# Decode attention and MLP, forward and backward, in one kernel: slots at a multiple of 512 bytes, and the last pass in 133 steps

## The chip, the core and the metric

The kernel runs on one core of a Trainium2 chip. The time is the device time of one execution in microseconds (us); lower is better.

## The reference

Two layers of attention and two of an MLP alternate. Each adds to its input; weights and caches are shared by both layers. B = 2, one query per batch, D = 1024, 32 query heads of 128 that share 4 key/value heads, 16384 cached keys, F = 3584. All arrays are bfloat16. The kernel returns the output and the gradients of all inputs but `B_x`.

```python
def A(x, k_cache, v_cache, wq, wo):           # k, v: [2, 4, 16384, 128]
    q = (x @ wq).reshape(B, 1, 32, 128).transpose(0, 2, 1, 3)
    k, v = repeat(k_cache, 8, axis=1), repeat(v_cache, 8, axis=1)
    p = softmax(einsum("bhqd,bhkd->bhqk", q, k) * 128 ** -0.5)
    return einsum("bhqk,bhkd->bhqd", p, v).transpose(0, 2, 1, 3).reshape(B, 1, 4096) @ wo

def M(x, w1, b1, w2, b2):
    return gelu(layernorm(x) @ w1 + b1) @ w2 + b2

x = x + A(layernorm(x), ...); x = x + M(layernorm(x), ...)   # layer 0
x = x + A(layernorm(x), ...); x = x + M(layernorm(x), ...)   # layer 1
outputs: x, and the vjp of all that with grad_out:
  out_1 = dx, out_2 = dK, out_3 = dV (16.8 million elements each), out_4 = dwq,
  out_5 = dwo, out_6 = dw1, out_7 = db1, out_8 = dw2, out_9 = db2
```

## The kernel before

The program is recorded as a list of pieces (`emit`), each with the chunks of SBUF that it uses, and then run in that order (`Program.run`). A chunk is a megabyte of keys, values or weights, 8 KB in each of 128 partitions. It gets one of 15 slots (or a part of two large tiles, `e1` and `ds1`, while these are free); its load is issued on SP's DMA queue, in the order of first use, as soon as a slot is free. In the last pass three slots are split into halves and four are whole store buffers (`HALF_AT`, `FULL_AT`), so that eight are left for loads. Engines run their instructions in the order in which the pieces stand; they wait for one another by semaphores alone.

There are four passes over the cache: attention forward of layer 0 and 1, backward of layer 1, and backward of layer 0 (`attn_bwd` with `l == 0`, the last pass). A pass goes through 8 groups (batch and key/value head), each in 16 blocks of 1024 cached rows. In a backward pass a step `s` does one value block: `kblock` transposes it on DVE (`kT`, L482) and multiplies it with the gradient (`sc`, L495, two blocks later). When half of a group's blocks is there, `slope` (L977, L980) turns scores into their gradients `ds`, and `xc` (L530) exchanges them across partitions into `xt`. A key block is multiplied with `xt` by `direct` (L520) into `sb[0]`, `LAG_B` = 14 steps behind the value block. `dq_of` (L986) scales the sum into `dq_all`. Only in the last group of the last pass two key blocks are done in a step: steps 126 to 129 and 133 to 136.

The last pass also makes all large outputs. `kv_outputs` writes the gradients of keys and values of both layers at once: eight products of 512 columns (L1180) for each megabyte, from `blk`, a transposed piece of `e` or `ds` (L1162). `dw_units` writes the weight gradients in products of 512 columns (L1234), between rows that `x_rows` (L1218) and `y_rows` (L1198, L1199) have set up in `X` and `Y`. Every product goes into a PSUM bank that `ob()` hands out in turn, `st["ob"] % 3` of `obanks`, and is cast into a store buffer by ACT (L236) or DVE (L239), whichever has less work on the planner's account (`cast_out`). When a buffer is full, POOL's queue issues its store (L1185, L1260).

`outputs(s, ...)` says which of these pieces a step gets: those of `kv_outputs` have their steps, the weight gradients stand in a list `bg`, of which a credit per step takes some. `wq_last_ops` turns the last two chunks of `wq` (L399) and multiplies them with `dq` (L412); `attn_in_bwd` is the backward layer norm (L600 to L616), and `col_to_row` (L562 to L564) writes its result, `out_1`. In the last pass these stand at steps 130 to 142, and steps go on to 149 until nothing is left.

In the forward passes `wo_fwd_blocks` (L648) multiplies the last heads' output with two chunks of `wo`, five steps after the last value chunk's first use.

Of the kernel before, what the change touches and what calls it, by code (L numbers as in the profile page):

```python
# [28 lines left out]
LAG_B = 14  # L29

# [111 lines left out]
def kernel(  # L142
# [71 lines left out]
    def ob():  # L214
        st["ob"] += 1
        return obanks[st["ob"] % 3]
# [337 lines left out]
    def col_to_row(colT, dram_out):  # L554
        c = P.chunk(kind="half")

        def f():
# [6 lines left out]
            GP.dma_start(dram_out, row)  # L564
# [94 lines left out]
    def attn_fwd(l, order, x_in, mark, behind=()):  # L659
# [94 lines left out]
        for i, k in enumerate(kvs):  # L754
# [4 lines left out]
            for n, b in enumerate(wo_fwd_blocks(l, k, xn, i == HKV - 1, acc_x)):  # L759
                at(32 * i + 33 + LAG_F + (n if i + 1 < HKV else 0), *b)  # L760
# [196 lines left out]
    def attn_bwd(l, order, gT, wo_first, outputs=None, mark=None, extra=None):  # L957
# [44 lines left out]
        for pos, g in enumerate(order):  # L1002
            for f in range(2):
                at(16 * pos + 10 + 8 * f, slope(pos, g, f))
                at(16 * pos + 11 + 8 * f, xc(pos, g, f))
            at(137 if l == 0 and pos == G - 1 else 16 * pos + LAG_B + 16, dq_of(pos, g))
# [7 lines left out]
        for i, k in enumerate(kvs):  # L1014
# [16 lines left out]
            else:  # L1031
# [3 lines left out]
                for n, b in enumerate(ops):  # L1035
                    wb.setdefault((118 if l == 1 else 130) + n, []).append(b)

        kc, vc = {}, {}
        n_steps = 128 + LAG_B if l == 1 else 137
        k_at = {}  # L1040
        for v in range(128):
            fast = 126 + v % 16 // 2 if v % 16 < 8 else 129 + v % 16 // 2
            k_at.setdefault(fast if l == 0 and v >= 112 else v + LAG_B, []).append(v)
        s = 0
        while s <= n_steps or (outputs is not None and outputs(s, True)):
            pos, i = divmod(s, 16)
# [3 lines left out]
            fill = list(outputs(s, False)) if outputs is not None else []  # L1050
# [15 lines left out]
            if s < 128:  # L1066
                g = order[pos]
                if i % 4 == 0:
                    kc[0] = ld_kv("V", g, i // 4)
                c = kc[0]  # L1070

                kblock(c, i, scb[0], g, fill[:n] + mids + fill[n:2 * n])
            else:
                for fn, us in fill[:n] + mids + fill[n:2 * n]:
                    emit(fn, us)
                if pend:
                    emit(*pend.pop(0))
            for fn, us in wb.pop(s, []) + (extra or {}).pop(s, []) + fill[2 * n:]:
                emit(fn, us)
            if s == n_steps:  # L1080
                aflush()
                parts = attn_in_bwd(l, gT, dnq)
                if l == 1:
                    for b in tail + parts:
                        emit(*b)
                else:
# [452 lines left out]
```

## Time and profile before

| | us |
|---|---|
| runs before | 1167.36, 1169.02, 1169.89; median 1169.02 |
| the profiled execution, its own time | 1169.38 |
| its span in the trace | 1167.6 |
| busy: PE, DVE, ACT, POOL | 830.9, 770.4, 488.8, 183.4 |
| moved by DMA | 356.5 MB read, 98.6 MB written |

The profile is of one execution. PE is TensorE's matmuls and PEld its weight loads, DVE is VectorE, ACT ScalarE, POOL GpSimd, SP the queue that issues loads. `x16` counts instructions that follow each other; L520 is line 520 of the kernel. Line numbers in the profile are those of the kernel before; in the kernel after, the same lines stand up to eleven further down. The share of the DMA engines counts the time that packets took, as a part of 16 engines' time, and can exceed 1 where packets overlap.

### The profile page before, as it was taken

The numbers are of one execution on the slowest core, as the hardware profiler recorded it, in microseconds if no ns is written. First come the engines' busy times: TensorE is split into PE (matmuls) and PEld (weight loads), VectorE is DVE, ScalarE is ACT, GpSimd is POOL, SyncE is SP. The second block draws the span as 40 slices with busy tenths as digits, with TensorE's granted clock in tenths as the row PEclk, the third lists the DMA queues.
The fourth block names the chain that finished last, engine by engine and source line by source line (L and its number), as shares of the span: only waits on it lengthen the run. The fifth ranks groups of instructions, "written<-read, shape, count | busy, mean of one in ns | idle before, by whom it ended". The sixth has DMA issues, their size and how long they took to land. (4 is left out here: it accounts for less than half of the span.)

```text
span 1167.6 us, 34350 instructions
## 1 busy us (share of the span) xinstructions
PE 830.9 (71%) x14751; PEld 621.6 (53%) x14761; DVE 770.4 (66%) x1490; ACT 488.8 (42%) x1128; POOL 183.4 (16%) x578
## 2 busy tenths in 40 slices
PE   5665565457886546888777578879666987798875
PEld 4554564456775445777767465444333444444443
DVE  5764673269886536664656465979566977787875
ACT  0422223002423221244444206758455866676773
POOL 1000000010000000110111101423222332333341
PEclk9999999999999555577877657989887989798997
DMA  9999999989999999999999997999999999999995
GB/s 356 412 414 414 413 420 410 405 319 413 410 414 414 414 399 356 405 414 412 409 414 412 377 341 275 340 405 424 401 358 407 420 415 381 425 421 399 392 419 218
DMA packets 99636, 457.37 MB, mean 392 GB/s; under 512 B 7668, under 2 KB 11778, under 8 KB 60188
## 3 DMA queue, kind: packets, MB, share of 16 engines
q1 hardware_dynamic: 81660, 356.56, 76.6%
q0 software_dynamic: 17824, 98.63, 20.7%
q8 instruction: 115, 1.88, 0.6%
q14 instruction: 37, 0.30, 0.1%
HBM read 356.54 MB, written 98.62 MB: 390 GB/s over the span
## 5 line engine op out<-in xcount | busy, mean ns | idle before, releaser
L482 DVE STREAM_TRANSPOSE kT<-slot 128x512 int32<-128x512 int32 x480 | 322.3, 694 | 130.3 <-PE sc L495 91.1
L495 PE MATMUL sc<-qbd,kT 128*128 128x32 bf16 x4096 | 264.7, 223 | 14.4 <-DVE kT L482 11.2
L495 PEld LDWEIGHTS <-kT 128*128 128x128 bf16 x4096 | 210.5, 115 | 59.1 <-issue 27.1
L520 PEld LDWEIGHTS <-slot 128*128 128x128 bf16 x3648 | 148.4, 103 | 131.7 <-issue 48.7
L236 ACT CAST slot<-sc 128x512 bf16<-128x512 f32 x332 | 189.0, 593 | 66.2 <-PE sc L1234 32.5
L520 PE MATMUL sb<-xt,slot 128*128 128x8 bf16 x3648 | 165.9, 177 | 65.3 <-DMA slot<-in_A_v_cache_dram 28.9
L239 DVE CAST slot<-sc 128x512 bf16<-128x512 f32 x187 | 126.2, 681 | 37.2 <-PE sc L1180 18.8
L1180 PE MATMUL sc<-slot,blk 128*128 128x512 bf16 x335 | 129.6, 405 | 25.7 <-DVE slot L239 8.4
L711 ACT ACTIVATE e<-sc 128x512 bf16<-128x512 f32 x32 | 19.0, 597 | 253.9 <-DVE sc L708 182.1
L236 ACT CAST slot<-sb 128x512 bf16<-128x512 f32 x169 | 100.0, 592 | 47.6 <-PE sb L1180 27.0
L530 POOL COPY xt<-ds 32x64 int32<-32x64 int32 x368 | 84.7, 230 | 192.1 <-DVE ds L980 155.9
L402 ACT COPY slot<-tp 128x512 int32<-128x512 int32 x96 | 55.2, 586 | 139.8 <-PE tp L399 138.3
L399 PE MATMUL tp<-ident,slot 128*128 128x128 bf16 x832 | 81.4, 264 | 18.0 <-DMA slot<-in_A_wq_dram 12.0
L1180 PEld LDWEIGHTS <-blk 128*128 128x128 bf16 x512 | 45.0, 99 | 69.4 <-issue 57.3
L1180 PE MATMUL sb<-slot,blk 128*128 128x512 bf16 x170 | 68.8, 405 | 17.8 <-DVE slot L239 13.1
L399 PEld LDWEIGHTS <-slot 128*128 128x128 bf16 x832 | 66.9, 121 | 21.9 <-DMA slot<-in_A_wq_dram 12.8
L530 ACT COPY xt<-e 32x128 int32<-32x128 int32 x256 | 75.6, 295 | 3.9
L239 DVE CAST slot<-sb 128x512 bf16<-128x512 f32 x96 | 65.0, 677 | 16.6 <-DMA out_dram<-slot 7.1
L1185 POOL DMA_DIRECT2D out_dram<-slot x64 | 35.3, 551 | 215.7 <-ACT slot L236 178.8
L384 DVE STREAM_TRANSPOSE slot<-slot 128x1024 int32<-128x1024 int32 (+1 forms) x48 | 55.2, 1178 | 15.3 <-DMA slot<-in_A_wq_dram 8.1
L1234 PE MATMUL sc<-slot,X 128*128 128x512 bf16 x157 | 60.7, 407 | 5.5 <-DVE slot L239 3.3
L587 POOL TENSOR_TENSOR m_rstd<-ln_vpe,neghalf 128x2 f32<-128x2 f32 x2 | 1.4, 716 | 374.2 <-DVE ln_vpe L585 374.2
(282 smaller groups left out, 932.9 us busy)
## 6 DMA issues: line engine op xcount, KB each, us to landing
slot<-in_A_k_cache_dram SPq DMA_DIRECT2D x114, 1024.0 KB, 14.4
slot<-in_A_v_cache_dram SPq DMA_DIRECT2D x109, 1024.0 KB, 13.4
out_dram<-slot POOLq DMA_DIRECT2D x64, 1024.0 KB, 11.3
slot<-in_A_wq_dram SPq DMA_DIRECT2D x31, 1024.0 KB, 12.5
slot<-in_A_wo_dram SPq DMA_DIRECT2D x27, 1024.0 KB, 12.5
out_dram<-slot POOLq DMA_DIRECT2D x54, 512.0 KB, 12.5
slot<-in_B_w_dram SPq DMA_DIRECT2D x22, 896.0 KB, 11.0
slot<-in_B_w_dram SPq DMA_DIRECT2D x11, 1024.0 KB, 11.4
```

Source lines behind the costliest of these rows:

```text
L236: S.copy(out=dst, in_=src)
L239: V.tensor_copy(out=dst, in_=src)
L384: V.transpose(out=t.ap[:, h * nw * 256:(h + 1) * nw * 256].bitcast(I32).rearrange("p (w j m) -> p w j m", j=4, m=32), in_=c.ap[:, 0:4 * nc ...
L399: PE.transpose(tp[:, j * 128:(j + 1) * 128], c.ap[:, off + j * 128:off + (j + 1) * 128], ident[:])
L402: S.copy(out=d.bitcast(I32), in_=tp.bitcast(I32))
L482: V.transpose(out=kT[:].bitcast(I32).rearrange("p (w j m) -> p w j m", w=4, j=4), in_=c.ap[:, (i % 4) * 1024:(i % 4 + 1) * 1024].bitcast(I ...
L495: PE.matmul(sc[:, a0:a0 + 4, :, 2 * (i % 4) + q], lhsT=kv[:, 2 * q + w, :, e], rhs=qbd[:, g, 2 * w + e], start=(w == 0 and e == 0), stop=( ...
L520: PE.matmul(acc, lhsT=c.ap[:, n * 128:(n + 1) * 128], rhs=xv[:, i // 4, t // 2, :, 2 * (i % 4) + t % 2], start=(fresh and i == 0 and t == ...
L530: (GP.tensor_copy if on[t % len(on)] == "g" else S.copy)(out=d[32 * t:32 * t + 32, c0:c0 + cn, j, :], in_=s[32 * j:32 * j + 32, c0:c0 + cn ...
L1180: PE.matmul(ps, lhsT=hold["blk"][:, j, :], rhs=flat(qm(w)[:, (u % 2) * 4:(u % 2) * 4 + 4, :]), start=True, stop=True)
L1185: GP.dma_start((dKv if w == 0 else dVv)[g, :, c * 32:(c + 1) * 32, :], stg.ap.rearrange("p (t d) -> p t d", d=128))
L1234: PE.matmul(ps, lhsT=hold[j // 4 * 4][:, j % 4, :], rhs=Y.ap[:, y_at + c0:y_at + c0 + cn], start=True, stop=True)
```

## The change

- **Slots.** `dbias` no longer has an SBUF tile of its own (144 bytes a partition): it uses one named `g_a` that exists. Everything allocated behind it moves down by 160 bytes, so that the first slot starts at byte 104,448 of a partition, a multiple of 512, where it was 104,608.
- **Two blocks a step.** In the last pass the last group's 16 value blocks are done in steps 112 to 119, two a step; its keys in 126 to 133 without the gap; `slope` and `xc` of that group at 117, 118, 122 and 123; its key gradients from step 124; `wq` is turned from step 121.
- **The end.** Steps end at 133 (`N_END`). What is left then is written out in one order by hand: `dq` and its rows, then pieces of the last key gradients, the `wq` products, the weight gradients and the layer norm between each other. `out_1` is stored from SP's queue instead of POOL's, and the layer norm's sums use a part of `sb[0]`.
- **Five banks.** From step 122 on, `obanks` also holds the two banks of the scores.
- **The weight gradients.** The credit changes its constants; the last two sets of `wq` gradients share their `X` rows (`hold_n`); `Y` is cleared before the pass begins, and the rows of `gA_all` are set up only ahead of `out_5`.
- **Forward.** The last two chunks of `wo` are asked for (an empty piece that uses them) one step before the last value chunk.

```diff
 LAG_B = 14
+N_END = 133
...
         st["ob"] += 1
-        return obanks[st["ob"] % 3]
+        return obanks[st["ob"] % len(obanks)]
...
-    def col_to_row(colT, dram_out):
+    def col_to_row(colT, dram_out, queue=None):
         c = P.chunk(kind="half")
...
                 V.tensor_copy(out=row[:, j0 * 128:(j0 + 4) * 128], in_=flat(ps))
-            GP.dma_start(dram_out, row)
+            (queue or GP).dma_start(dram_out, row)
...
             acc_x = (lambda: x_in()[:]) if i == 0 else (lambda: xn[:])
-            for n, b in enumerate(wo_fwd_blocks(l, k, xn, i == HKV - 1, acc_x)):
+            blocks = wo_fwd_blocks(l, k, xn, i == HKV - 1, acc_x)
+            if i + 1 == HKV:
+                at(123 + LAG_F, lambda: None, blocks[0][1])
+            for n, b in enumerate(blocks):
                 at(32 * i + 33 + LAG_F + (n if i + 1 < HKV else 0), *b)
...
         for pos, g in enumerate(order):
+            quick = l == 0 and pos == G - 1
             for f in range(2):
-                at(16 * pos + 10 + 8 * f, slope(pos, g, f))
-                at(16 * pos + 11 + 8 * f, xc(pos, g, f))
-            at(137 if l == 0 and pos == G - 1 else 16 * pos + LAG_B + 16, dq_of(pos, g))
+                n = 117 + 5 * f if quick else 16 * pos + 10 + 8 * f
+                at(n, slope(pos, g, f))
+                at(n + 1, xc(pos, g, f))
+            at(N_END + 1 if quick else 16 * pos + LAG_B + 16, dq_of(pos, g))
         dnq = wrk.tile([128, DJ, 2], F32, name="dnq")
...
                 for n, b in enumerate(ops):
-                    wb.setdefault((118 if l == 1 else 130) + n, []).append(b)
+                    wb.setdefault((118 if l == 1 else 121) + n, []).append(b)
         kc, vc = {}, {}
-        n_steps = 128 + LAG_B if l == 1 else 137
-        k_at = {}
+        n_steps = 128 + LAG_B if l == 1 else N_END
+        k_at, v_at = {}, {}
         for v in range(128):
-            fast = 126 + v % 16 // 2 if v % 16 < 8 else 129 + v % 16 // 2
-            k_at.setdefault(fast if l == 0 and v >= 112 else v + LAG_B, []).append(v)
+            quick = l == 0 and v >= 112
+            k_at.setdefault(126 + v % 16 // 2 if quick else v + LAG_B, []).append(v)
+            v_at.setdefault(112 + v % 16 // 2 if quick else v, []).append(v)
         s = 0
-        while s <= n_steps or (outputs is not None and outputs(s, True)):
-            pos, i = divmod(s, 16)
+        while s <= n_steps:
             if s == 10 and mark is not None:
...
             pre = list(ev.pop(s, ()))
-            fill = list(outputs(s, False)) if outputs is not None else []
+            fill = list(outputs(s)) if outputs is not None else []
             mids = []
...
                 emit(fn, us)
-            if s < 128:
-                g = order[pos]
+            between = fill[:n] + mids + fill[n:2 * n]
+            for v in v_at.get(s, ()):
+                pos, i = divmod(v, 16)
                 if i % 4 == 0:
-                    kc[0] = ld_kv("V", g, i // 4)
-                c = kc[0]
-
-                kblock(c, i, scb[0], g, fill[:n] + mids + fill[n:2 * n])
-            else:
-                for fn, us in fill[:n] + mids + fill[n:2 * n]:
-                    emit(fn, us)
-                if pend:
-                    emit(*pend.pop(0))
+                    kc[0] = ld_kv("V", order[pos], i // 4)
+                kblock(kc[0], i, scb[0], order[pos], between)
+                between = []
+            for fn, us in between:
+                emit(fn, us)
+            if s not in v_at and pend:
+                emit(*pend.pop(0))
             for fn, us in wb.pop(s, []) + (extra or {}).pop(s, []) + fill[2 * n:]:
                 emit(fn, us)
-            if s == n_steps:
-                aflush()
-                parts = attn_in_bwd(l, gT, dnq)
-                if l == 1:
-                    for b in tail + parts:
-                        emit(*b)
-                else:
-                    for n, b in enumerate(tail):
-                        wb.setdefault(138 + n // 4, []).append(b)
-                    for n, b in enumerate(parts):
-                        wb.setdefault(140 + n, []).append(b)
+            if l == 0 and s == 122:
+                emit(lambda: obanks.extend([half[0, 0], half[0, 1]]))
             s += 1
+        aflush()
+        parts = attn_in_bwd(l, gT, dnq)
+        if l == 1:
+            todo = tail + parts
+        else:
+            rows, kv_units, units = outputs(s, True)
+            todo = ev.pop(s) + rows + kv_units[0:2] + tail[0:4] + kv_units[2:4] + tail[4:] + units[0:2] + parts[0:1]
+            todo += units[2:4] + parts[1:2] + units[4:7] + parts[2:] + units[7:] + kv_units[4:]
+        for b in todo:
+            emit(*b)
         assert not ev and not wb and not pend and not extra, (ev, wb, extra)
...
             h["dn"] = dn
-            h["ps"] = ln_bwd_sums(dn[:], vec_y[f"a{l}"][:], half[0, 0])
+            h["ps"] = ln_bwd_sums(dn[:], vec_y[f"a{l}"][:], half[0, 0] if l == 1 else sb[0][:, 200:])
+            dve(0.8)
...
             V.tensor_tensor(out=gn[:], in0=dx[:], in1=gT()[:], op=ALU.add)
+            dve(1.3)
             if l == 1:
...
         if l == 0:
-            res.append(col_to_row(saved["gA0"], out_1.rearrange("b s d -> (b s) d")))
+            res.append(col_to_row(saved["gA0"], out_1.rearrange("b s d -> (b s) d"), nc.sync))
         return res
...
             at_ = max(base + 4 * c, 3) if w == 1 else base + 14 + 4 * c
+            if w == 0 and pos == G - 1:
+                at_ = 124 + 3 * c
             stg = P.chunk(kind="full")
...
-    def dw_units(xn, q, y_at, pieces):
-
-        hold = {}
+    def dw_units(xn, q, y_at, pieces, hold=None):
+
+        built = set() if hold is None else {0, 1}
+        hold = {} if hold is None else hold
         todo = []
...
                 todo.append((j, (f, [stg, Y])))
-        res, built = [], set()
+        res = []
         for n, (_, u) in enumerate(todo):
...
         def f():
-            s = wrk.tile([128, FJ + DJ], F32, name="dbias", bufs=1)
+            s = flat(wrk.tile([128, FJ, 2], F32, name="g_a")[:])[:, 0:FJ + DJ]
             V.tensor_reduce(out=s[:, 0:FJ], in_=dh_all[:], axis=AX.X, op=ALU.add)
...
             ps = ob()[0:FJ + DJ, 0:128]
-            PE.transpose(ps, s[:], identf[:])
+            PE.transpose(ps, s, identf[:])
             V.tensor_copy(out=c.ap[0:FJ + DJ, 0:128], in_=ps)
...
     emit(g1_, ws_o)
+    emit(lambda: V.memset(Y.ap, 0.0), [Y])
     extra = {4: [(spread_a0, ())], 9: [col_to_row(xM1, out_0.rearrange("b s d -> (b s) d"))]}
...
             sched.setdefault(s_, []).append((fn, us))
-    early = [(lambda: V.memset(Y.ap, 0.0), [Y]), y_rows(gM_all, 0, 8, 0, 0), y_rows(gA_all, 0, 8, 0, 1024)]
+    early = [y_rows(gM_all, 0, 8, 0, 0)]
     units = dw_units("h", 0, 0, pieces_rows(out_8, F, D))
...
     early += dw_units("m", 1, 0, pieces_rows(out_6, D, F))
-    early += dw_units("o", 0, 1024, pieces_rows(out_5, HQ * DH, D))
+    early += [y_rows(gA_all, 0, 8, 0, 1024)] + dw_units("o", 0, 1024, pieces_rows(out_5, HQ * DH, D))
     late = {}
+    hold_n = {}
     for i in range(HKV):
...
         rows = [y_rows(dq_all, k * R, 8, 2, k * 1024)]
-        units = dw_units("n", 2, 0, pieces_rows(out_4, D, 1024, k * 1024))
-        if i + 1 < HKV:
-            late[16 * (2 * i + 1) + LAG_B + 17] = rows + units
-        else:
-            late[133] = [u for u in units if not u[1]]
-            late[137] = rows + [u for u in units if u[1]]
+        units = dw_units("n", 2, 0, pieces_rows(out_4, D, 1024, k * 1024), hold_n if i + 2 >= HKV else None)
+        if i + 2 == HKV:
+            units = [x_rows("n", 4 * h, 4, 2, hold_n) for h in range(2)] + units
+        late[16 * (2 * i + 1) + LAG_B + 17 if i + 1 < HKV else N_END + 1] = rows + units
     bg = list(early)
     state = {"credit": 0.0}
-    END = 150
     STAGE = set(HALF_AT + FULL_AT)
-    def outputs(s, ask):
-        if ask:
-            return s < END or bool(bg) or any(x >= s for x in sched)
+    def outputs(s, rest=False):
+        if rest:
+            fin = late.pop(s)
+            return fin[0:1], sum([sched.pop(x) for x in sorted(sched)], []), bg + fin[1:]
         if s in STAGE:
...
             bg.extend(late.pop(s))
-        state["credit"] += max(1.3, len(bg) / (126 - s)) if s < 120 else 4
+        state["credit"] += max(1.3, len(bg) / (128 - s)) if s < 124 else 3
         while bg and state["credit"] >= 1:
```

## The prediction

> **What bounds the kernel now.** I read the page's slices first, then busy time by stage, then the end instruction by instruction.
>
> ```profile
> span 1167.6 us, 34350 instructions
> ...
> DMA  9999999989999999999999997999999999999995
> GB/s 356 412 414 414 413 420 410 405 319 413 410 414 414 414 399 356 405 414 412 409 414 412 377 341 275 340 405 424 401 358 407 420 415 381 425 421 399 392 419 218
> ```
>
> Each slice is 29.2 us. The DMA engines are busy in nearly all of them; they stand idle in a few (319, 275, 218 GB/s). Time can be won where bytes do not flow. The stages that matter, in one answer (us of window; its length; busy us of PE, PEld, DVE, ACT, POOL; then granted clock, DMA share, GB/s):
>
> ```profile
> 20.00:660.00 640.00, 427.16 (x9615) 389.83 (x9616) 387.10 (x794) 179.28 (x508) 34.08 (x145) 0.86 1.01 404
> 660.00:720.00 60.00, 39.97 (x865) 34.60 (x862) 32.37 (x69) 15.66 (x39) 3.30 (x14) 0.57 0.87 324
> 720.00:1074.00 354.00, 283.17 (x3265) 150.48 (x3265) 273.59 (x473) 236.02 (x464) 115.37 (x333) 0.90 0.98 398
> 1074.00:1100.00 26.00, 22.58 (x248) 11.18 (x247) 22.83 (x34) 18.56 (x37) 8.87 (x24) 0.94 0.94 364
> 1100.00:1143.00 43.00, 35.86 (x483) 21.03 (x484) 32.52 (x55) 31.45 (x68) 14.70 (x45) 0.96 1.02 420
> 1143.00:1163.00 20.00, 12.91 (x119) 6.70 (x117) 11.84 (x27) 7.79 (x14) 4.00 (x7) 0.82 0.56 220
> 1163.00:1167.60 4.60, 0.00 (x0) 0.00 (x0) 0.00 (x0) 0.00 (x0) 0.04 (x1) 0.50 0.01 1
> ```
>
> The last pass begins at about 708 us. It is held by DMA up to 1143 (share 0.94 to 1.02). Then come 20 us at share 0.56, in which no engine is full either (DVE 11.84 of 20, ACT 7.79): a chain of dependent work. At 420 GB/s those 20 us could have carried 8.4 MB and carried 4.4, so idle DMA worth 20 x (1 - 220/420) = 9.5 us lies there. This is the most that any reordering of the end can win.
>
> **The end, step by step.** The rows are start us, us, engine, line, instruction, and in brackets the idle time before and its releaser.
>
> ```profile
> 1142.29 0.58 PE L520 MATMUL sb<-xt,slot 128*128 128x8 bf16 x16
> ...
> 1144.04 0.17 DVE L986 TENSOR_SCALAR dq_all<-sb 128x8 bf16<-128x8 f32 x1
> ...
> 1144.90 0.69 DVE L1199 COPY slot<-sc 4x1024 bf16<-4x1024 bf16 x1 [0.56 <-PE sc L1198]
> ...
> 1145.64 0.58 PE L1234 MATMUL sc<-slot,X 128*128 128x512 bf16 x1 [0.78 <-DVE slot L1199]
> ...
> 1146.27 0.58 ACT L236 CAST slot<-sc 128x512 bf16<-128x512 f32 x1 [3.59 <-PE sc L1234]
> ...
> 1158.51 0.58 ACT L236 CAST slot<-sc 128x512 bf16<-128x512 f32 x1 [1.88 <-PE sc L539]
> ...
> 1162.50 0.53 POOL L564 DMA_DIRECT2D out_dram<-slot  x1 [2.40 <-DVE slot L563]
> ```
> ```profile
> L236 ACT CAST slot<-sc 128x512 bf16<-128x512 f32 x10 | 5.9, 588 | 7.7 <-PE sc L1234 5.3 <-PE sc L539 1.9 <-PE sc L1180 0.5
> L239 DVE CAST slot<-sc 128x512 bf16<-128x512 f32 x6 | 4.2, 692 | 1.5 <-PE sc L1234 1.1
> ...
> L239 DVE CAST slot<-sb 128x512 bf16<-128x512 f32 x4 | 2.8, 690 | 0.4 <-PE sb L1234 0.2
> L236 ACT CAST slot<-sb 128x512 bf16<-128x512 f32 x4 | 2.4, 588 | 0.9 <-PE sb L1234 0.7 <-PE sb L1180 0.2
> ```
>
> The last key block ends at 1142.29 + 0.58 = 1142.9. Its `dq` is scaled (L986), turned into rows (L1198, L1199), and the first weight-gradient product starts at 1145.64; ACT has waited 3.59 us for it. Then 24 casts (10 + 6 + 4 + 4) run from 1146.27 to 1158.51 + 0.58 = 1159.1, one in 0.53 us. ACT at 588 ns and DVE at 692 together could do one in 1/(1/0.588 + 1/0.692) = 0.318 us. Three banks feed them, and a bank comes back only after product, cast and two handovers. The layer norm and the row of `out_1` then follow alone, to 1162.50, and the span ends 1167.6 - 1162.5 = 5.1 us later.
>
> **The change part by part.**
>
> *The tail.* In the built order of the changed kernel 22 casts follow the last key block (6 of the last key gradient, 16 of `wq`), against 24. The six stand inside the `dq` chain, so 1142.9 to 1145.64 is no longer empty. The layer norm and the row go between the `wq` products, the row's store goes to SP's queue, behind which nothing is left, and five banks turn. DVE has besides its casts L986 and L1199 (0.17 + 0.69), eleven small layer-norm operations which I estimate at the 0.17 of L986 (1.9), and two row casts which I take at a cast's 0.69 (1.4): 4.1 us. With a casts on ACT, 0.588a = 0.692(22 - a) + 4.1 gives a = 15.1, or 8.9 us. The six early casts fill 6 x 0.318 = 1.9 of the chain's 2.8 us; the other 0.9 stays empty. The last cast ends at 1142.9 + 8.9 + 0.9 = 1152.7, the last store is issued some 0.4 later, and it is a large one:
>
> ```profile
> out_dram<-slot POOLq DMA_DIRECT2D x4, 512.0 KB, 3.2
> out_dram<-slot POOLq DMA_DIRECT2D x1, 4.0 KB, 1.6
> ```
>
> It lands 3.2 - 1.6 = 1.6 us later than the small row did. So the span ends at 1153.1 + 5.1 + 1.6 = 1159.8, that is **7.8 us earlier**, provided that the last key block stays where it is. Bounds: nothing, if DMA still sets the end, and the 9.5 from above.
>
> *Two blocks a step.* The last group's 16 value blocks take steps 112 to 119, its keys 126 to 133, the `slope` work 117 and 122. No instruction is added; order alone moves.
>
> ```profile
> 1074.11 0.71 DVE L482 STREAM_TRANSPOSE kT<-slot 128x512 int32<-128x512 int32 x1
> ...
> 1103.54 0.70 DVE L482 STREAM_TRANSPOSE kT<-slot 128x512 int32<-128x512 int32 x1
> ```
> ```profile
> SPq L325 <- DVE kT L482: 19.9, 3, 9.1
> ```
>
> These are value blocks 112 and 120: eight steps in 29.4 us, 3.7 a step. In these eight steps the changed order consumes two value megabytes more than before. At 420 GB/s that is 2 x 1.049/0.42 = 5.0 us, and the eight later blocks are then relieved of it. SP waits for slots already (the row is that wait from 1040 to 1130). Waiting behind a late value block are DVE's `kT` and all casts queued behind it, so the gradient banks, so PE. But the built order hands SP the last two value chunks four steps, 14.7 us, ahead (before: four and six); and its last key load is handed out with 78 casts left instead of 52, so loads end sooner. I take **+2.0**, nearer to nothing than to the 5.0; bounds 0 and +5.0. The wait for `slope`'s scores moves forward with the blocks and costs nothing of its own.
>
> *The start of the pass.* `Y`'s memset and one of the two `y_rows` leave the first step.
>
> ```profile
> 705.60 0.17 DVE L927 TENSOR_TENSOR dof<-sb,rbc 128x16 f32<-128x16 f32 x1 [4.38 <-PE sb L412]
> ...
> 709.09 1.76 DVE L1457 MEMSET slot<- 128x2048 uint32 x1 [0.38 <-issue]
> ```
> ```profile
> 711.12 1.01 PE L1198 MATMUL sc<-ident,gM_all 128*4 128x128 bf16 x8
> 711.93 1.06 PE L1198 MATMUL sc<-ident,gA_all 128*4 128x128 bf16 x8
> 712.92 0.64 PE L1162 MATMUL tp<-ident,e 128*64 128x128 bf16 x8
> ```
>
> The memset goes into the 4.38 us in which DVE waited. It was covered by PE's own queue at 709, so its 1.76 us go for nothing; the second row of transposes held PE from 711.93 to 712.92. **-0.9**, bounds 0 and -2.7 (memset too). DMA is not full there (0.87), so this shifts the pass.
>
> *Forward passes.* The last `wo` load is asked for before the last value chunk.
>
> ```profile
> 205.81 1.02 PE L520 MATMUL sb<-xt,slot 128*128 128x8 bf16 x32 [1.03 <-DMA slot<-in_A_v_cache_dram]
> ```
> ```profile
> 211.09 1.76 PE L648 MATMUL tp<-o_all,slot 128*128 128x2 bf16 x60 [2.39 <-DMA slot<-in_A_wo_dram]
> ```
>
> The same three loads must land; the value products (1.0 us) and `out_of` (an estimated 0.6) now follow the last of them, +1.6 us on a path with loads queued behind it: **0**, bounds -1.6 and +1.6. The credit for background units (128 for 126) leaves 151 casts at block 112 instead of 147: **0**, within the 26 x (1 - 364/420) = 3.5 us that one lull like 1074:1100 costs, in either direction.
>
> *Slots at a multiple of 512.* Slot 0 starts at byte 104,608 of a partition before, 160 over a multiple of 512, and at 104,448 after. No slot of this trace is aligned, so I bound it. The first answer is 110:124 (value and key loads), the second 1000:1020 (loads and stores mixed):
>
> ```profile
> DMA packets 819, 5.88 MB, mean 420 GB/s; under 512 B 89, under 2 KB 89, under 8 KB 106
> ```
> ```profile
> DMA packets 1308, 8.50 MB, mean 425 GB/s; under 512 B 143, under 2 KB 143, under 8 KB 399
> ```
>
> Unaligned slots reach 425 where the engines have both kinds of work. If alignment gave loads that rate everywhere, the 640 us of the first window row would shrink by 640 x (1 - 420/425) = 7.5. I take **0**, since the same slots already show 425; bounds -7.5 and, as nothing is made longer, 0.
>
> The Trainium skill, "DMA: Bandwidth & Descriptors", section "How a descriptor splits into AXI transactions", says that a descriptor starting off a 256-byte boundary starts fetching at the boundary below and pays beats for the unused bytes. By its figures an 8 KB row read from such a slot would take an estimated 261 beats for 256, 2% more. No run here has an aligned slot to show it; 425 GB/s in a mixed stretch of unaligned stores does not look like it.
>
> Sum: -7.8 + 2.0 - 0.9 = -6.7 us. The profiled execution took 1169.38 (span 1167.6), which gives 1162.7; the median of the runs, 1169.02, lies 0.4 below it, so **1162.3**.
>
> **The rivals.**
>
> *Slower: value blocks outrun their loads.* If two blocks a step wait for DMA, DVE's casts stand behind `kT`, stores dry up, and the pass has another lull. Price: the 5.0 us of two more loads, 3.5 of a lull, and half of the tail's gain (3.9), because casts left behind crowd it: 1169.0 - 0.9 - 3.9 + 8.5 = **1172.7**. It decides from about 5 us of `kT` waiting for value loads between blocks 112 and 127. For it: SP's 19.9 us. Against: the four steps' lead.
>
> *No change: DMA keeps the end.* Share 1.02 up to 1143 means that a denser tail only waits longer for its stores: 1169.0 - 0.9 = **1168.1**. Against: share 0.56 behind it.
>
> *Aligned rows flow faster* all over: 1162.3 - 7.5 = **1154.8**. For it: 420 against 425. Against: as above. The page named there would have this case, too.
>
> **How the numbers follow.** Forecast 0.60 (own range 1158 to 1167), slower 0.18, no change 0.10, alignment 0.12. This kernel's runs differ by about 0.2%, 2.3 us, so faster means below 1166.7. Of the forecast 0.57 lies there and 0.03 at the edge; of no change 0.02 and 0.08: faster 0.57 + 0.02 + 0.12 = 0.71, same 0.03 + 0.08 = 0.11, slower 0.18. The range 1156 to 1171.5 leaves out most of the alignment case and two thirds of the slower one.
>
> **What would show it.** Right: the last key block near 1141 to 1145, no ACT wait of 3 us behind it, casts one in 0.32 to 0.40 us, a DMA share over 0.75 in its last 15 us. The start shows one `y_rows` before the first scores. Wrong: `kT` waits for value loads over 5 us; or the stage 20:660 shortens by several us, which would be the slots; or the last key block comes at 1150.

## The result, and the profile after

| | us |
|---|---|
| before, runs of the same chip | 1167.36, 1168.52, 1169.02, 1169.89; median 1168.77 |
| after | 1150.88, 1151.50, 1152.69, 1152.78; median 1152.1 |
| ratio | 0.9857, interval 0.9840 to 0.9874 |
| the profiled execution after, its own time and span | 1150.88 and 1149.1 |

The forecast was 1162.3 and the range 1156.0 to 1171.5. The sign was right. The time lies below the range, nearest to the rival to which I gave 0.12 (aligned rows flow faster, 1154.8).

The page of the kernel after: its span, and the slices of DMA, 28.7 us each.

```profile
span 1149.1 us, 34357 instructions
...
DMA  9999999989999999999999997899999999999997
GB/s 361 421 421 422 422 425 418 411 316 421 418 423 422 422 405 351 415 421 422 418 422 420 382 339 300 305 395 425 419 346 419 424 420 387 420 422 423 381 422 292
```

Before, most full slices of the first half stood at 409 to 414; now most stand at 418 to 425. In the second half the fullest slices stood at 420 to 425 already.

The windows of the kernel after. The third row is the last pass, from its first scores' transpose to the last key block, and the fourth what follows it. The last row is the last 15 us:

```profile
20.00:649.00 629.00, 423.78 (x9594) 386.30 (x9595) 386.82 (x793) 179.24 (x508) 34.09 (x145) 0.92 1.01 411
300.00:400.00 100.00, 70.91 (x1559) 63.27 (x1557) 74.41 (x149) 29.60 (x90) 0.00 (x0) 1.00 1.02 422
695.80:1127.70 431.90, 348.18 (x4075) 188.16 (x4084) 333.96 (x565) 294.30 (x592) 138.66 (x402) 0.91 0.97 394
1127.70:1149.10 21.40, 10.84 (x102) 5.58 (x102) 9.44 (x24) 6.96 (x13) 3.46 (x5) 0.71 0.61 249
1134.10:1149.10 15.00, 6.49 (x22) 2.49 (x20) 6.07 (x14) 4.30 (x8) 2.91 (x4) 0.61 0.47 193
```

And of the kernel before, the 48.5 us ahead of the last pass, the last pass, and what follows it:

```profile
659.40:707.90 48.50, 30.13 (x799) 28.57 (x796) 25.88 (x60) 7.58 (x21) 3.30 (x14) 0.55 0.96 357
707.90:1142.90 435.00, 351.96 (x4069) 189.22 (x4078) 336.03 (x570) 294.10 (x585) 138.84 (x402) 0.90 0.97 392
1142.90:1167.60 24.70, 13.01 (x120) 6.80 (x119) 11.84 (x27) 7.79 (x14) 4.13 (x7) 0.76 0.46 181
```

In the kernel before, the windows are divided where the last key block ends (1142.9). In this and all later profiles they are divided some 0.4 us behind that end, which is at 1127.3 in the kernel after. From end to end, then: of the 18.5 us between the two profiles, 707.9 - 695.8 = 12.1 lie ahead of the last pass, in a stretch whose instructions the change hardly touches. 435.0 - 431.5 = 3.5 lie in the last pass and 24.7 - 21.8 = 2.9 behind it. I had put 7.8 on the last of these three parts, a loss of 2.0 on the second, and 0.9 on the first.

The end of the kernel after, from its timeline (start, us, engine, line, instruction; in brackets the idle time before and its releaser):

```profile
1126.70 0.57 PE L521 MATMUL sb<-xt,slot 128*128 128x8 bf16 x16
...
1131.67 0.59 PE L1245 MATMUL sc<-slot,X 128*128 128x512 bf16 x2
...
1133.33 0.59 PE L540 MATMUL sb<-lb_s,onesf 128*128 128x4 f32 x2 [1.06 <-DVE lb_s L604]
1133.78 0.59 PE L1245 MATMUL sb<-slot,X 128*128 128x512 bf16 x1
1134.16 1.91 PE L1245 MATMUL sc<-slot,X 128*128 128x512 bf16 x4
...
1136.46 0.17 DVE L1117 TENSOR_TENSOR gA<-lb_dx,gM 128x16 f32<-128x16 f32 x1
1136.78 1.01 PE L563 MATMUL sb<-identf,gA 128*2 128x128 f32 x4 [0.71 <-DVE gA L1117]
1137.59 1.06 PE L563 MATMUL sc<-identf,gA 128*2 128x128 f32 x4
...
1138.44 1.49 PE L1245 MATMUL sc<-slot,X 128*128 128x512 bf16 x3
...
1139.29 2.56 DVE L240 CAST slot<-sc 128x512 bf16<-128x512 f32 x4
...
1139.54 0.59 ACT L237 CAST slot<-sc 128x512 bf16<-128x512 f32 x1 [2.72 <-PE sc L1245]
...
1140.24 0.59 ACT L237 CAST slot<-sb 128x512 bf16<-128x512 f32 x1
...
1140.72 1.08 ACT L237 CAST slot<-sc 128x512 bf16<-128x512 f32 x2
...
1141.77 0.68 DVE L240 CAST slot<-sb 128x512 bf16<-128x512 f32 x1
...
1143.00 0.72 POOL L1271 DMA_DIRECT2D out_dram<-slot  x1 [0.47 <-issue]
```

The last key block ends at 1127.3. The last cast ends at 1142.45, 15.2 us later, where I had summed 9.8. From the first product of `wq` to the last of its sixteen casts it takes 1131.67 to 1142.45, 0.67 us a cast, although five banks turn. By this timeline it is PE that holds them up: its queue is in order, and it stands 1.06 us for the layer norm's sums, then 0.71 us for the gradient, and then spends 1137.59 + 1.06 - 1136.78 = 1.87 us on the four-byte transposes of the `out_1` row. Products of `wq` are queued behind each of these. Behind the row, where PE waits for nothing more, the last nine casts take 1139.29 to 1142.45, 0.35 us each, and that is the pace that I had forecast for all of them.

### The profile page after: what moved, and what is told of

Same layout as the page of the kernel before. It is cut to its first block, busy times and chain, and to the rows that moved or that the text cites. A ratio compares the mean times of both kernels' runs of the same rounds, so it can differ in the third digit from the quotient of the medians.

```text
span 1149.1 us, 34357 instructions
## 1 busy us (share of the span) xinstructions
PE 822.2 (72%) x14742; PEld 616.5 (54%) x14753; DVE 768.1 (67%) x1483; ACT 488.1 (42%) x1133; POOL 182.6 (16%) x577
## 3 DMA queue, kind: packets, MB, share of 16 engines
q0 software_dynamic: 17792, 98.62, 20.7%
## 4 chain that ended last, share of the span: by engine, by line
PE 27%; DMA 22%; DVE 15%; issue 5%; ACT 4%; POOL 1%; SPq 0%; DVEq 0%; POOLq 0%; ACTq 0%
DMA out_dram<-slot 5%; PE sc L496 5%; DMA slot<-in_A_wq_dram 5%; DMA slot<-in_A_v_cache_dram 5%; DMA slot<-in_A_k_cache_dram 4%; DVE slot L240 4%; DVE kT L483 4%; PE tp L400 4%; PE sc L1190 3%; PE sb L521 3%; ACT slot L237 3%; PE sb L413 2%; DMA slot<-in_A_wo_dram 2%; DVE slot L385 2%; PE sc L1245 2%
## 5 line engine op out<-in xcount | busy, mean ns | idle before, releaser
L240 DVE CAST slot<-sc 128x512 bf16<-128x512 f32 x197 | 131.6, 679 | 32.9 <-PE sc L1245 11.9
L403 ACT COPY slot<-tp 128x512 int32<-128x512 int32 x100 | 57.5, 587 | 135.9 <-PE tp L400 134.6
L237 ACT CAST slot<-sb 128x512 bf16<-128x512 f32 x158 | 93.3, 590 | 39.6 <-PE sb L1190 17.4
L240 DVE CAST slot<-sb 128x512 bf16<-128x512 f32 x92 | 62.3, 677 | 12.5 <-PE sb L1190 6.4
L1271 POOL DMA_DIRECT2D out_dram<-slot x62 | 41.9, 676 | 160.0 <-ACT slot L237 108.3
```

What stands on the lines that cost most here:

```text
L237: S.copy(out=dst, in_=src)
L240: V.tensor_copy(out=dst, in_=src)
L403: S.copy(out=d.bitcast(I32), in_=tp.bitcast(I32))
L1271: GP.dma_start(out_ap[j0 * 128:(j0 + rb) * 128, c0 + cb:c0 + cb + cn].rearrange("(j p) n -> p j n", p=128), ap[:, 0:rb * cn].rearrange("p ...
```

## The experiments

Times are medians; "ratio" is to the kernel before, with its 95% interval. The kernels of one group were run on the same chip together with the kernel before: a1 to a4; d0, b1, c1 and c3; a5, c5, e1 and e2; c4, c7 and c8. The medians of the kernel before were 1168.7, 1169.6, 1167.9 and 1169.4 in these groups, so across groups it is the ratios that compare.

### What a slot's first byte is worth

An unused tile shifts what is allocated behind it, the slots included; the instructions and their order stay as they are:

```diff
+    pers.tile([128, 88], F32, name="pad")     # 352 bytes; 40, 24, 104, 120 words in the others
     Et = [pers.tile(
```

> The kernel before with one unused tile of 352 bytes a partition ahead of the `e` tiles, so that slot 0 starts at a multiple of 512 bytes (104,960) instead of 160 beyond one (104,608). Nothing else differs; the order of every instruction is that of before. Theory A (alignment lets loads flow faster wherever loads alone run): the loads' 8 KB packets take 309 ns instead of 316 in the first 650 us, the third pass ends about 10 us earlier, the last pass starts about 12 us earlier, the end keeps before's shape (24.7 us from the last key block), and the time is 1155 to 1159 us. Theory O (the new order of the last pass and of its start made the gain, and slots cost nothing): 1167 to 1170.

> The changed kernel with one unused tile of 160 bytes a partition ahead of the `e` tiles, so that slot 0 starts 160 bytes beyond a multiple of 512, as before the change. The order is that of the changed kernel. Theory A: 8 KB packets at 316 ns again, last pass starts near 707 us, time 1162 to 1166 (only the order's part of the gain, 4 to 6 us, is left; my prediction's 1162.3 would then have been the order's worth). Theory O: 1150 to 1154.

> The kernel before with 96 bytes of padding: slot 0 at a multiple of 256 bytes that is not one of 512. If the boundary that counts is 256 bytes or smaller (the skill's rule), this is as good as 512: 1155 to 1159 and 309 ns for 8 KB. If it must be 512: 1167 to 1170 and 316 ns.

> The kernel before with 416 bytes of padding: slot 0 at 64 bytes beyond a multiple of 512. If 64 bytes suffice: 1155 to 1159, 309 ns. If any offset off the boundary costs one more piece of each row, whatever its size: 316 ns and 1167 to 1170. If the cost grows with the bytes below the start (2 beats of 32 bytes for 64, 5 for 160, by the rule of the Trainium skill, DMA: Bandwidth & Descriptors, How a descriptor splits into AXI transactions): two fifths of the 6.6 ns, 311 to 312 ns, and 1160 to 1163.

> The kernel before with 480 bytes of padding: slot 0 at 128 bytes beyond a multiple of 512. If the boundary is 256 bytes (as the skill's page states; 64 and 160 beyond it cost the full price, 256 none): 8 KB packets at 315 to 316 ns and 1167 to 1171. If 128 bytes suffice: 309 ns and 1153 to 1157.

| kernel | slot 0, bytes past a multiple of 512 | 8 KB load packet, mean ns, 20 to 640 us | GB/s, 300 to 400 us | last pass begins | time | ratio |
|---|---|---|---|---|---|---|
| before | 160 | 315.5 | 413 | 707.9 | 1168.7 | 1 |
| before, padded (a4) | 64 | 315.6 | 412 | 708.3 | 1169.9 | 1.0010 (0.9998 to 1.0021) |
| before, padded (a5) | 128 | 315.0 | 413 | 706.4 | 1170.5 | 1.0018 (1.0007 to 1.0029) |
| before, padded (a3) | 256 | 310.5 | 422 | 694.6 | 1155.2 | 0.9878 (0.9862 to 0.9894) |
| before, padded (a1) | 0 | 310.5 | 422 | 693.9 | 1154.7 | 0.9875 (0.9858 to 0.9891) |
| after, padded (a2) | 160 | 315.7 | 413 | 707.8 | 1165.5 | 0.9971 (0.9959 to 0.9983) |
| after | 0 | 310.6 | 422 | 695.8 | 1152.1 | 0.9857 (0.9840 to 0.9874) |

The packet times are from the records of the load queue; a packet is one row of 8 KB here. The kernel before with aligned slots (a1), in the same windows as above:

```profile
300.00:400.00 100.00, 70.38 (x1543) 62.87 (x1541) 73.88 (x149) 29.61 (x90) 0.00 (x0) 0.50 1.02 422
693.90:1130.90 437.00, 354.37 (x4082) 189.54 (x4081) 335.96 (x570) 293.89 (x585) 138.88 (x402) 0.90 0.97 392
1130.90:1154.10 23.20, 11.72 (x116) 5.88 (x114) 11.77 (x27) 7.68 (x14) 3.96 (x6) 0.81 0.44 183
```

And with slots 64 bytes past the boundary (a4):

```profile
300.00:400.00 100.00, 71.11 (x1547) 63.25 (x1547) 75.00 (x153) 31.12 (x96) 0.00 (x0) 1.00 1.02 412
708.30:1146.80 438.50, 354.04 (x4081) 190.16 (x4080) 335.86 (x570) 293.65 (x585) 138.92 (x402) 0.90 0.97 390
```

Theory A holds, and O falls: the pad alone gives 0.9875, and taking alignment away from the changed kernel brings it back to 0.9971. Three things follow. The boundary is 256 bytes: 256 is as good as 512, while 128 and 64 gain nothing (why 128 came out 0.18% above the kernel before isn't known). The price doesn't grow with the offset: 64 bytes cost as much as 160. And it is paid where loads run alone: a1 begins its last pass 14.0 us earlier than before. The pass itself, with stores between the loads, gains nothing: up to the end of the last key block it takes 436.6 and 434.8 us with aligned slots (a1, a3) against 435.0, 438.1 and 434.4 without (before, a4, a5). There 86 to 91 in a hundred load packets take 309 ns in every one of these kernels, aligned or not. Where loads run alone, 99 in a hundred do with aligned slots, and 8 to 32 without.

The granted clock in these rows is 0.50 in a1 and 1.00 in a4, and the aligned one is the faster: TensorE's clock has no part in it. The Trainium skill, "DMA: Bandwidth & Descriptors", section "How a descriptor splits into AXI transactions", names the 256-byte boundary, and the runs agree with it. What it says is about reading from an unaligned start, though, while these loads write to the slots, and the 8 KB packets of the last pass's stores, which do read from slots, take 311 to 314 ns in the mean with aligned slots and 312 to 315 without. So the runs agree on the boundary, and do not show that its mechanism is the one at work. It also lets the cost grow with the bytes between boundary and start (an estimated 258 beats for 256 at 64 bytes, 261 at 160); the 315.6 ns at 64 beside 315.5 at 160 speak against that.

### What the order is worth

a2 has the whole new order on the old slots: 0.9971, that is 3.4 us less than before (2.0 to 4.8). On aligned slots the intervals of the old order (a1, a3) and the new one overlap. The order's parts were undone one by one in the kernel after, whose second set of runs is d0:

> The changed kernel once more, unchanged, as the measure for the variants of it that follow: 1150.5 to 1153.5.

One block a step again (c1) and three banks (b1); c8 has both. The lines with which c1 and c8 set `slope`, `xc`, the key gradients and the turning of `wq` back to their old steps are not shown:

```diff
-N_END = 133
+N_END = 137
...
-            k_at.setdefault(126 + v % 16 // 2 if quick else v + LAG_B, []).append(v)
-            v_at.setdefault(112 + v % 16 // 2 if quick else v, []).append(v)
+            fast = 126 + v % 16 // 2 if v % 16 < 8 else 129 + v % 16 // 2
+            k_at.setdefault(fast if quick else v + LAG_B, []).append(v)
+            v_at.setdefault(v, []).append(v)
...
-                emit(lambda: obanks.extend([half[0, 0], half[0, 1]]))
+                pass
```

> The changed kernel with the last group's values again one block a step, its keys, slopes, key gradients and `wq` products at the steps of before, and 137 steps; the aligned slots, the new order behind the last step, the five banks (from step 131) and the new start stay. By my prediction two blocks a step cost 2.0 us, so this is 1149 to 1151. Rival: with them loads are asked for earlier, and they gained what the last pass gained up to its last key block (431.3 us from its first scores' transpose, against 436.4 in the kernel before with aligned slots): 1155 to 1158.

> The changed kernel with three PSUM banks for gradients all the way (the two more are not handed over at step 122). My prediction took the pace of 0.53 us a cast from three banks; if that holds, the 22 casts behind the last key block take about 3 to 4 us more: 1155 to 1157. Theory P (TensorE's queue paces the tail): 1152 to 1153.5.

> The changed kernel with one block a step and three banks: both undone at once. If the two parts work only together (five banks carry the casts that two blocks a step pile up before the last key block, and two blocks a step leave fewer casts behind it): 1155 to 1157, as with either one undone. If their costs add (4.3 + 5.3 us): 1160 to 1163.

| kernel | last pass, us | behind it, us | time | ratio |
|---|---|---|---|---|
| after, again (d0) | 433.7 | 20.9 | 1151.3 | 0.9845 (0.9827 to 0.9863) |
| one block a step (c1) | 434.2 | 23.9 | 1155.6 | 0.9890 (0.9871 to 0.9909) |
| three banks (b1) | 439.9 | 20.1 | 1156.6 | 0.9891 (0.9873 to 0.9909) |
| both (c8) | 434.8 | 23.9 | 1156.3 | 0.9889 (0.9873 to 0.9906) |

The windows of b1, and the ends of d0 and c1:

```profile
695.80:1135.70 439.90, 352.69 (x4075) 189.10 (x4084) 334.92 (x565) 295.15 (x592) 138.91 (x402) 0.90 0.96 389
1135.70:1155.80 20.10, 9.27 (x101) 4.64 (x102) 9.45 (x24) 7.09 (x13) 3.46 (x5) 0.94 0.51 210
...
1129.40:1150.30 20.90, 10.97 (x102) 5.41 (x102) 9.64 (x25) 7.14 (x13) 3.46 (x5) 0.74 0.64 266
...
1129.30:1153.20 23.90, 11.20 (x115) 5.69 (x114) 10.46 (x26) 8.40 (x15) 3.48 (x5) 0.78 0.49 203
```

The two parts work only together. Undoing either, or both, gives the same time, and it is close to that of the aligned kernel before (0.9875). So the rest of the new order, the order by hand behind the last step included, shows no gain without these two. The places differ: with three banks the last pass is 6.2 us longer and the end isn't; with one block a step the pass is as it was and the end is 3.0 us longer. So c1's time falls within the rival's range, but not for the rival's reason, which was a longer pass. POOL's issues show where the 3.0 us are. In d0 the last store of key gradients, 1 MB (L1195), is out early, and a store of `wq` is last:

```profile
1133.87 0.55 POOL L1195 DMA_DIRECT2D out_dram<-slot  x1 [4.85 <-ACT slot L237]
...
1144.65 0.72 POOL L1271 DMA_DIRECT2D out_dram<-slot  x1 [0.73 <-issue]
```

In c1 four products of keys are still to be done behind `wq`, and the megabyte comes last:

```profile
1144.44 0.73 POOL L1272 DMA_DIRECT2D out_dram<-slot  x1 [0.47 <-ACT slot L237]
1145.65 0.57 POOL L1196 DMA_DIRECT2D out_dram<-slot  x1 [0.48 <-issue]
```

From the key block (1129.4 and 1129.3) the last issue is 1.1 us later, and from there the span ends after 7.5 us instead of 5.7, which together are the 3.0. (The order behind the last step is made for two blocks a step; another one might have put the keys first in c1 too. That wasn't tried.) The two further banks earn their keep ahead of the last key block, where the work of two blocks a step crowds them, and not in the tail, for which I had counted them. My price for two blocks a step has the wrong sign in this company. What I feared, `kT` waiting for value loads, doesn't occur. Here is the group of the sixteen transposes in the kernel after, 1060 to 1093.1; the last column is the idle time before them:

```profile
L483 DVE STREAM_TRANSPOSE kT<-slot 128x512 int32<-128x512 int32 x16 | 11.0, 695 | 0.9 <-PE sc L496 0.8
```

The old start of the pass:

```diff
-    emit(lambda: V.memset(Y.ap, 0.0), [Y])
...
-    early = [y_rows(gM_all, 0, 8, 0, 0)]
+    early = [(lambda: V.memset(Y.ap, 0.0), [Y]), y_rows(gM_all, 0, 8, 0, 0), y_rows(gA_all, 0, 8, 0, 1024)]
```

> The changed kernel with `Y`'s memset and the row of `gA` back in the first step of the last pass. By my prediction 0.9 us more (bounds 0 and 2.7), 1152.5 to 1153.5. By the profiles, in which the time from the third pass's last transpose to the last pass's first is 46.3 to 46.8 us with the new start and 46.3 to 46.4 with the old one on aligned slots: nothing, 1151 to 1152.5.

1151.5, ratio 0.9843 (0.9823 to 0.9864), where d0 has 0.9845: nothing that these runs can tell, though their intervals are too wide to exclude 0.9 us. The profile of this run begins its last pass at 695.1, d0's at 695.7.

### What paces the end

The row last (c3) moves one term of the order, and the stores' queue (c4, e1) one argument:

```diff
-            todo += units[2:4] + parts[1:2] + units[4:7] + parts[2:] + units[7:] + kv_units[4:]
+            todo += units[2:4] + parts[1:2] + units[4:] + parts[2:] + kv_units[4:]
...
-                GP.dma_start(out_ap[j0 * 128:(j0 + rb) * 128,
+                (queue or GP).dma_start(out_ap[j0 * 128:(j0 + rb) * 128,
```

> The changed kernel with the four-byte transposes that make the row of `out_1`, its casts and its store behind the last `wq` product instead of four products into them. Theory P (the tail is paced by TensorE's queue: 0.71 us of waiting for VectorE and 2.07 us of transposes stand ahead of nine products): the last store is issued 1.5 to 2.5 us earlier, 1149 to 1151. Theory C (my prediction: ACT's and DVE's casts set the pace): nothing is won, and the row's chain stands alone at the end, 1152 to 1154.

> The changed kernel with the last group's four `wq` stores on SP's queue alone, the row of `out_1` where the change put it, so that SP's queue holds three of the stores behind the row's. In the profiles the span ended 3.0 us after the last byte of a large store of POOL's queue, and 1.4 after one of SP's. If that is all: 1.6 us less plus POOL's issues of 0.72 us, about 1149 to 1150. If both edits are needed: 1151 to 1152.

> The changed kernel with the row of `out_1` behind the last `wq` product and the last group's four `wq` stores issued by SP, whose queue is empty there, instead of POOL. In the kernel with the row last alone, POOL issued the last store at 1142.55, 0.56 us after its last cast, and the span ended 5.65 us later. If SP issues sooner and its descriptors need not be written by POOL: 0.5 to 1.5 us below that kernel, 1148 to 1149.5. If landing costs the same from either queue: 1149.5 to 1150.5.

The sums in two parts (e2, which has both edits above as well):

```diff
-tail[4:] + units[0:2] + parts[0:1]
-            todo += units[2:4] + parts[1:2] + units[4:7] + parts[2:] + units[7:] + kv_units[4:]
+tail[4:] + parts[0:1] + units[0:4]
+            todo += parts[3:4] + units[4:8] + parts[1:2] + units[8:] + parts[2:3] + kv_units[4:]
```

> As the kernel before it (row last, SP's stores), and the layer norm's sums in two parts: VectorE's part ahead of the first `wq` product, TensorE's four products later, the rest of the layer norm after eight, so that TensorE never stands waiting for VectorE with products behind it. Nothing is left out. Theory P: another 1.0 us (the 1.07 us of waiting), 1147 to 1148.5. Theory C: the same time as the kernel before it.

And the layer norm and the row left out (c5):

> The changed kernel without the layer norm and the row behind the last key block: `out_1` is stored early in the pass from another tile, so its eleven small VectorE operations, TensorE's sums and eight four-byte transposes and the two row casts are left out of the tail. Theory P (TensorE's queue paces the tail: 1.07 us waiting for the sums' input, 0.84 waiting for the gradient and 2.07 of transposes stand ahead of `wq` products): 3.5 to 4.2 us less, 1147 to 1148.5. Theory C (casts on ACT and DVE at full speed, my prediction's sum, 0.588a = 0.692(22 - a) + 0.9 in place of + 4.1): 1.5 us less, 1150 to 1151.

| kernel | behind the last key block, us | granted clock there | time | ratio |
|---|---|---|---|---|
| after, again (d0) | 20.9 | 0.74 | 1151.3 | 0.9845 (0.9827 to 0.9863) |
| row last (c3) | 19.1 | 0.72 | 1150.1 | 0.9838 (0.9821 to 0.9855) |
| stores on SP (c4) | 18.5 | 0.82 | 1150.9 | 0.9837 (0.9815 to 0.9858) |
| both (e1) | 17.5 | 0.71 | 1147.2 | 0.9816 (0.9799 to 0.9833) |
| both, and sums in two parts (e2) | 15.9 | 0.87 | 1146.8 | 0.9816 (0.9800 to 0.9831) |
| layer norm left out (c5) | 16.7 | 0.86 | 1149.6 | 0.9842 (0.9824 to 0.9860) |

The lengths of the end are from one profile each, and for the end they are the sharper measure: the times also hold what the last pass does, which differed by up to 5 us among profiles of this order (430.1 in c7's, 435.5 in c5's). They differ with the granted clock, too: with the same order behind the last step a2, c7, d0 and the kernel after have ends of 20.6, 20.7, 20.9 and 21.4 us at clocks of 0.83, 0.81, 0.74 and 0.71. By these lengths theory P holds. Without the layer norm and the row the end is 4.2 us shorter than d0's, and 4.0 shorter than that of c7, whose clock is nearer; P said 3.5 to 4.2 and my own sum 1.5. c5's total does not show it, since its last pass came out 1.8 us longer than d0's. Moving the row alone gives 1.8 at nearly the same clock. From e1 to e2, which splits the sums, it is another 1.6, but e2's clock was 0.87 and e1's 0.71, so part of that may be the clock's. By the totals alone c3, c4 and c5 aren't told from the kernel after, nor e2 from e1. e1 came out below both of its expected ranges, c5 between its two.

In e2 the end has become what I had drawn for the kernel after:

```profile
1133.36 0.17 DVE L1118 TENSOR_REDUCE lb_s<-lb_t 128x2 f32<-128x16 f32 x1
...
1133.59 0.39 PE L540 MATMUL sb<-lb_s,onesf 128*128 128x4 f32 x2
1133.61 0.59 ACT L237 CAST slot<-sb 128x512 bf16<-128x512 f32 x1
1133.83 0.81 PE L1256 MATMUL sc<-slot,X 128*128 128x512 bf16 x3
1134.24 2.54 ACT L237 CAST slot<-sc 128x512 bf16<-128x512 f32 x5
```

```profile
1128.70:1144.60 15.90, 8.49 (x102) 4.62 (x102) 9.09 (x24) 6.71 (x13) 0.55 (x1) 0.87 0.82 332
```

PE's sums no longer wait, ACT casts five in a row at 0.51 us, and the DMA share of the end is 0.82, from 0.61. By their ratios e1 and e2 lie 3.4 us below d0 and 4.8 below the first runs of the kernel after; their intervals overlap that of d0 by less than 0.1% and lie wholly below that of the first runs.

The other part of e1 is the queue. The last 6 us of the kernel after, whose last large store POOL issued, and the last 6 us of e1, in 40 slices of 0.15 us:

```profile
DMA  1999999992599999998100000000000000000000
```

And e1:

```profile
DMA  8102999999994699999999999999996000000000
```

After POOL's store the bytes stop 20 slices before the end of the span, 3.0 us; after SP's, 9 slices, 1.35 us. The queue alone (c4) makes the end 2.2 us shorter than c7's at nearly the same clock, although three `wq` stores stand in SP's queue behind the row's there and are issued only from 1142.91 on. Its time isn't told from d0's.

## Why the prediction was wrong, and where it was right

**Slots at a multiple of 512: 0 taken, bounds -7.5 and 0; about -14 measured.** This is the step that failed, and alone it puts the time outside the range. By a1 it is 1 - 0.9875 of 1168.7, 14.6 us (12.7 to 16.6); by a2 against the kernel after, 13.3. Two errors made it. First, I took 420 GB/s for the unaligned rate from one window of 14 us (110 to 124), though most of the full slices that I had quoted above it show 409 to 414. The window's loads are in rows of 8 KB alone, and there the aligned kernels move 425 and 427 GB/s (a1, after): 420 was the unaligned rate of that mix, and not what it would reach anyway. With the 425 that I allowed, the bound would have been 640 x (1 - 413/425) = 18 us, and the range would have held the result. Second, I argued that unaligned slots reach 425 "where the engines have both kinds of work", and took this as a sign against the cost. It was true, and it spoke of the other stage: mixed with stores the load packets lose nothing, alone they lose 5 ns of 310.5 in the mean. A rate seen in one mix of traffic says nothing of another. The means 315.5 and 310.5 differ by 1.6% and the rates 413 and 422 by 2.2%. The 2% that I had worked out from the rule of the Trainium skill is near that, and I had set it aside by that same argument.

**The tail: -7.8, bounds 0 and -9.5; about -3 measured** (from the end of the last key block 24.7 us before, and 24.7 and 23.6 with the old order on aligned slots, a3 and a1; 21.8 and 21.3 in the two profiles after, and 21.0 in a2). With one block a step again the end is 24.3 (c1), so these 3 us hang on the two blocks as well. The step that failed is the line 0.588a = 0.692(22 - a) + 4.1. It let ACT and DVE set the pace and gave PE no term at all. PE is busy for 10.84 of that window's 21.4 us only, but its queue is in order, and twice it waits for DVE with products behind it. So the casts came one in 0.67 us and not in 0.32 to 0.40, and the DMA share of the last 15 us is 0.47 where I had looked for over 0.75. The last issue came 15.7 us behind the key block and not 10.2.

**Two blocks a step: +2.0, bounds 0 and +5.0.** Wrong in sign: undone, it costs 5 us (0.9845 to 0.9890), and those bounds excluded a gain. The profiles place 3.0 of these in the end, where c1's megabyte of keys comes last, so part of them may belong to an order that was made for two blocks a step. I priced what it does to loads and looked for the wait at `kT`, which isn't there. I left out that the last key gradients move ahead with the blocks, so that their megabyte is issued 16 us before the end (1133.87 of 1150.3 in d0) and not last, and that it takes five banks to carry them.

**The start: -0.9.** Not seen (c7). **Forward `wo`: 0**, not tried by itself. With it and aligned slots the third pass ends at 648.0 to 649.6 in eleven profiles; without it at 647.5 and 648.2 (a1, a3). So it may have cost about 1 us, within the bounds of 1.6, and it shows no gain. **The credit: 0**, not tried.

**The order as a whole: -6.7; -3.4 measured** on the old slots (a2), -2.1 to -3.5 on aligned ones by the ratios of a1, of the kernel after and of d0, whose intervals overlap. So two errors of opposite sign, a tail half as good and two blocks a step better than feared, left a smaller one, and that they did so is luck.

**The rivals.** The one that held is the alignment, to which I gave 0.12. Its time, 1154.8, came near by luck: it took 7.5 us for the slots, about half of what they gave, and 6.7 for the order, about twice what it gave. That value blocks outrun their loads is refuted by the 0.9 us of idle time before `kT`. That DMA keeps the end is refuted by its share of 0.61 there. What I named as the sign of the slots' part, a first stage shorter by several us, is what the windows show: from 20 us on to the end of the third pass it takes 629 us, where it took 640.

## What to carry to other kernels

Where loads run alone and DMA is the bound, look at the address of the tiles they land in before anything else: here some hundred bytes of padding to a multiple of 256 gave 1.25%, four times what the whole new order gave. Bound an effect on a rate by the stage's own rate over its whole length, and not by a short window or by another mix of traffic. And when the end of a kernel is costed by its casts, write down what the in-order queue of the engine that feeds them has to wait for.

## What the runs showed of the hardware

Where loads run alone (20 to 640 us), a load of 8 KB rows into SBUF takes 310.5 to 311.0 ns a packet, in the mean, to a multiple of 256 bytes, and 315.0 to 315.7 to 64, 128 or 160 bytes past one; the 2 KB packets of the same queue take 86 against 89. That the cost vanishes between stores was not expected, and what hides it there isn't shown. Nor was it that the span ends 3.0 us after the last byte of a large store of POOL's queue (after, d0, a2, b1, c1, c3, c5, c7, c8) and 1.3 to 1.4 after one of SP's (c4, e1, e2).
